# Second product of the last tile pair as seven block products, with the combined weights prepared through DRAM

## Chip, cores, metric

One core of one Trainium2 chip runs the whole kernel. The metric is the device time of one launch in microseconds (us), lower is better. Engines are named as in the profile: PE is TensorE (PEld its weight loads), DVE VectorE, ACT ScalarE, POOL GpSimd, SP the engine that issues most DMAs.

## What is computed

Masked attention (8 batches, 8 heads, 576 positions of 64) gives, rearranged, a matrix `x` of 4608 rows by 512. Behind it stands a feed-forward block:

```python
x = attn_out.transpose(0, 2, 1, 3).reshape(B * S, H * D)      # 4608 x 512
h = x @ w_in                                                  # 512 -> 2048
g = h * np.clip(h + 3.0, 0.0, 6.0) / 6.0
out = (g @ w_out).astype(np.float32)                          # 2048 -> 512
```

`h = x @ w_in` is called the first product here and `g @ w_out` the second. All arithmetic is float32. A float32 product is made of three matmuls on operands that are split into a high part and a remainder: high·high, high·low, low·high.

## The kernel before

The 4608 rows are nine tiles of 512: one for each batch (its first 512 positions), and one, called `l`, that gathers the last 64 positions of all eight batches. Tiles 0 to 2 are done one at a time (`ffn`). The other six are done in three pairs, (3, 4), (5, 6) and (7, `l`), by `ffn_pair`. `w_out` in its two parts lies in DRAM scratch as `wod` and is loaded again for each tile, 512 KB for each of its 16 row blocks `fc`.

**First product of a pair.** For each `m` of 0 to 7, `pair_products(m)` makes the blocks `fc` = 2m and 2m+1 of both tiles together. Two tiles times two blocks are a 2 x 2 block product, and it is made by seven block products in place of eight: sums of the two tiles (`combine_x`, tiles `xc`) and sums of weight blocks (`combine_weights`, DRAM scratch `wid`) are made ahead, and `product(0)` to `product(6)` run in two PSUM banks `ph`, with the sums between them taken while the accumulation goes on: `copy` takes a bank to SBUF, `add` adds a bank to such a copy, and the next product accumulates on the bank that was copied. Each product is two groups of three matmuls of 512 columns (lines 1210 to 1212). `gate` makes `g` from a bank or a copy with one ACT and one DVE instruction.

**Second product of a pair.** Tile a's is made between the first products (`second(fc, ...)`, `mm2`, lines 970 to 972): for each `fc`, four groups of three matmuls of 512 columns, one group for each block of 128 rows, in the four banks `acc`. Its operand `g` is split by ACT (line 1003) and POOL (line 1006). Tile b's `g` is kept in SBUF, and its second product follows alone, with the same number of matmuls.

In the last pair (`ends`), the last four `fc` of the second tile (`BEHIND`) are held back so that the four row blocks end one after the other; each is scaled by 1/6 out of its bank (`output`, lines 982 and 984) and stored.

**What sets the order.** No order is written out. `op(...)` records a step with its engine or engines, an estimated duration, the keys that it reads and writes and a due time; `Plan.emit` then goes through all steps as a list scheduler and writes each engine's instructions in the order it found. Each engine runs its list strictly in that order, DMA queues too. So a step that is added can move others on every engine that it shares.

Of the kernel before, what the change touches and what calls it, by code (L numbers as in the profile page):

```python
# [10 lines left out]
F32 = mybir.dt.float32  # L11
# [41 lines left out]
SHORT = 3.05  # L53
LASTS = (16.6, 2.8)
BEHIND = 4
PLAIN = {0: (0, 0), 1: (2, 0), 5: (2, 1)}
# [151 lines left out]
def attention_ffn(ctx: ExitStack, tc, q, k, v, w_in, w_out, out):  # L208
# [19 lines left out]
    wod = dp.tile([NFC, P, 2, TOK], F32, name="wod")  # L228
    wid = dp.tile([7 * NFC // 4, P, 2, TOK], F32, name="wid")

    plan = Plan()
# [744 lines left out]

    def output(t, i, uk, make, rows, due, ends=False):

# [7 lines left out]
        def store():  # L986
            o = tiles[uk.key if isinstance(uk, Slot) else uk]
            for n, (to, part) in enumerate(rows):
                (nc.scalar if ends and n % 2 else nc.sync).dma_start(to, o[part])
        op({"ACT": 0.6, "DVE": 0.69}, 0, ob, reads=[("acc", i), "tmps"] if isinstance(uk, Slot) else [("acc", i)], writes=[uk], take=uk if isinstance(uk, Slot) else None, due=due - 4000)  # L990
# [6 lines left out]

    def split_g(fc, uk, gk, due, t, held=False):
        def to(x):
            return tiles[gk[x]] if held else new(gp, gk[x], [P, TOK], F32R, f"g{x}{t}_{fc}")  # L1000

# [166 lines left out]

    def ffn_pair(p):
        s0 = first[p]  # L1170
        ends = p == len(PAIRS) - 1
        long, short = LASTS if ends else (LONG, SHORT)
        half = s0 + HALVES * long
# [3 lines left out]
        def out_of(which, end):  # L1177
            def go(i):
                uk = Slot(tmps)
                output(names[which], i, uk, lambda: None, rows_of(PAIRS[p][which], i), end, ends=ends and which == 1)  # L1180
            return go
# [13 lines left out]
        def pair_products(m):  # L1195
# [35 lines left out]

            def gate(fc, which, src, reads, give, both):
                if which:
                    uk = kept_g[fc]
                    make = lambda: new(xp, uk, [P, TOK], F32, f"g{p}_{fc}")
                else:
                    uk = u_slot()
                    make = lambda: new(gp, uk, [P, TOK], F32, f"u{p}_{fc}")
# [19 lines left out]
            gate(f1, 1, lambda: tiles[banks[0]], [banks[0]], None, False)  # L1258

        for m in range(HALVES):  # L1260
            if m:
# [4 lines left out]
        second(NFC - 1, half - 0.2 * long)  # L1266
        behind = NFC - BEHIND
        for fc in range(NFC):
            at = half + fc * short
            gk = [("g", fc % 2, x) for x in range(2)]  # L1270
            if ends and fc >= behind:
                gk = [("ge", fc, x) for x in range(2)]

                def both(fc=fc, gk=gk):
                    t = new(wp, xc[fc - behind], [P, 2, TOK], F32R, f"ge{fc}")
                    for x in range(2):
                        tiles[gk[x]] = t[:, x]
                op("SP", 0.0, both, writes=[xc[fc - behind], *gk], due=at)
            split_g(fc, kept_g[fc], gk, at - 2000, names[1], held=ends and fc >= behind)
            when = [at + 0.2 * i * short for i in range(4)]  # L1280
            if ends and fc >= behind:
                when = [half + (behind + BEHIND * 0.25 * i + 0.01 * (fc - behind)) * short for i in range(4)]
            mm2(fc, gk, second_weights(fc, half + min(fc, behind) * short), when.__getitem__, names[1], None, out_of(1, half + NFC * short))

# [66 lines left out]
    for p, now in enumerate(PAIRS):  # L1351
        combine_x(p, first[p] - 30)
        ffn_pair(p)
        for b in PAIRS[p + 1] if p + 1 < len(PAIRS) else ():
# [44 lines left out]
```

## Time and profile before

| | before |
|---|---|
| device time, median of 3 runs | 898.61 us (897.04 to 899.19) |
| the profiled execution: its own time | 896.24 us |
| its span in the trace | 894.5 us |
| PE busy | 874.2 us (98%) |
| weight loads (PEld) busy | 705.3 us (79%) |
| DVE, ACT, POOL busy | 522.9, 378.5, 430.4 us |
| DMA | 191.17 MB, 214 GB/s on average |
| chain that ended last | PE 83%, DMA 7%, SP's queue 3%, DVE 3% |

The profile shows one execution. Its times count from the start of the span; the launch's own time is 1.7 us longer. A matmul's recorded length (0.39 us for 512 columns) is longer than the distance from one start to the next, because matmuls are pipelined. So the rate is read from starts, and a short wait of PE can be seen as a wider distance of two starts while the engine still counts as busy.

### The profile page before, as it was taken

The numbers are of one execution on the slowest core, as the hardware profiler recorded it, in microseconds if no ns is written. First come the engines' busy times: TensorE is split into PE (matmuls) and PEld (weight loads), VectorE is DVE, ScalarE is ACT, GpSimd is POOL, SyncE is SP. The second block draws the span as 40 slices with busy tenths as digits, with TensorE's granted clock in tenths as the row PEclk, the third lists the DMA queues.
The fourth block names the chain that finished last, engine by engine and source line by source line (L and its number), as shares of the span: only waits on it lengthen the run. The fifth ranks groups of instructions, "written<-read, shape, count | busy, mean of one in ns | idle before, by whom it ended". The sixth has DMA issues, their size and how long they took to land.

```text
span 894.5 us, 19609 instructions
## 1 busy us (share of the span) xinstructions
PE 874.2 (98%) x7760; PEld 705.3 (79%) x7760; DVE 522.9 (58%) x910; ACT 378.5 (42%) x673; POOL 430.4 (48%) x389
## 2 busy tenths in 40 slices
PE   9899999999999999999999999999999999999997
PEld 6577868878887877878888888888887888888786
DVE  6778866577876867775768704444576024444400
ACT  4686555343434334444345623344355223223320
POOL 6778677286766757232334945122258422112340
PEclk9999999999999999999999999999999999999999
DMA  8989998778989889997973695866746676555364
GB/s 196 296 187 173 258 344 218 176 211 205 244 209 249 230 214 208 282 232 195 226 213 131 240 277 170 267 192 206 218 129 245 232 232 195 198 187 193 127 213 131
DMA packets 219290, 191.17 MB, mean 214 GB/s; under 512 B 163520, under 2 KB 177856, under 8 KB 219200
## 3 DMA queue, kind: packets, MB, share of 16 engines
q1 hardware_dynamic: 218724, 189.12, 75.3%
q8 instruction: 61, 1.00, 0.5%
q10 hardware_dynamic: 476, 0.82, 0.3%
q14 instruction: 29, 0.24, 0.1%
HBM read 157.38 MB, written 32.51 MB: 212 GB/s over the span
## 4 chain that ended last, share of the span: by engine, by line
PE 83%; DMA 7%; SPq 3%; DVE 3%; POOL 2%; ACT 1%; issue 1%; ACTq 0%; DVEq 0%; POOLq 0%
PE ph L1210 9%; PE ph L1212 8%; PE ph L1211 8%; PE ph L1037 4%; PE acc L970 4%; PE acc L972 4%; PE ph L1039 4%; PE acc L971 4%; PE ph L1038 4%; PE ps L667 3%; DMA rawi<-in_moe_w_in_dram 2%; SPq L413 2%; PE pv L432 2%; PE acc0b L970 2%; PE acc0a L970 2%; PE acc0b L972 2%
## 5 line engine op out<-in xcount | busy, mean ns | idle before, releaser
L1210 PE MATMUL ph<-xc,wi 128*128 128x512 f32 x336 | 132.9, 396 | 0.1
L1212 PE MATMUL ph<-xc,wi 128*128 128x512 f32 x336 | 130.9, 389 | 0.0
L1211 PE MATMUL ph<-xc,wi 128*128 128x512 f32 x336 | 130.9, 389 | 0.0
L1229 DVE TENSOR_TENSOR htmp<-ph,htmp 128x512 f32<-128x512 f32 x72 | 49.6, 689 | 78.0 <-PE ph L1212 72.8
L1006 POOL TENSOR_TENSOR g<-u,g 128x512 fp32r<-128x512 f32 x48 | 63.4, 1320 | 40.2 <-ACT g L1003 27.9
L1037 PE MATMUL ph<-x,wi 128*128 128x512 f32 x192 | 77.7, 405 | 3.5 <-DVE u L1076 3.2
L972 PE MATMUL acc<-wo,g 128*128 128x512 f32 x192 | 75.1, 391 | 2.3 <-POOL g L1006 2.3
L970 PE MATMUL acc<-wo,g 128*128 128x512 f32 x192 | 77.2, 402 | 0.0
L1039 PE MATMUL ph<-x,wi 128*128 128x512 f32 x192 | 75.2, 392 | 0.6 <-POOL wi L363 0.6
L1038 PE MATMUL ph<-x,wi 128*128 128x512 f32 x192 | 75.1, 391 | 0.0
L971 PE MATMUL acc<-wo,g 128*128 128x512 f32 x192 | 74.9, 390 | 0.0
L1210 PEld LDWEIGHTS ph<-xc,wi 128*128 128x128 f32 x336 | 63.0, 188 | 14.2 <-DVE g L1076 0.6
L1212 PEld LDWEIGHTS ph<-xc,wi 128*128 128x128 f32 x336 | 63.1, 188 | 13.4
L1211 PEld LDWEIGHTS ph<-xc,wi 128*128 128x128 f32 x336 | 63.1, 188 | 12.4
L799 DVE STREAM_TRANSPOSE atloc<-e 32x192 f32<-32x192 f32 x168 | 61.9, 368 | 8.9 <-POOL e L758 5.2
L743 POOL TENSOR_TENSOR e<-e,st 128x288 f32<-128x288 f32 (+1 forms) x30 | 34.3, 1143 | 62.2 <-DVE st L721 62.1
L1072 ACT ACTIVATE u<-ph,three 128x512 f32<-128x512 f32 x48 | 33.0, 688 | 73.4 <-PE ph L1039 72.2
L1072 ACT ACTIVATE u<-htmp,three 128x512 f32<-128x512 f32 x48 | 34.7, 723 | 66.7 <-DVE htmp L1229 66.7
L1006 POOL TENSOR_TENSOR g12a<-u,g02a 128x512 fp32r<-128x512 f32 x14 | 18.1, 1292 | 84.4 <-ACT g02a L1003 84.4
L1006 POOL TENSOR_TENSOR g11a<-u,g01a 128x512 fp32r<-128x512 f32 x16 | 21.4, 1335 | 69.5 <-ACT g01a L1003 68.1
L1221 ACT COPY htmp<-ph 128x512 f32<-128x512 f32 x53 | 31.1, 588 | 42.4 <-PE ph L1212 42.0
L758 POOL TENSOR_TENSOR e<-e,st 128x288 f32<-128x288 f32 (+1 forms) x30 | 35.5, 1183 | 26.2 <-DVE st L754 25.7
(234 smaller groups left out, 2092.2 us busy)
## 6 DMA issues: line engine op xcount, KB each, us to landing
wo<-wod SPq DMA_DIRECT2D x128, 512.0 KB
wi<-wid SPq DMA_DIRECT2D x84, 512.0 KB
rawi<-in_moe_w_in_dram SPq DMA_DIRECT2D x16, 512.0 KB
rawo<-in_moe_w_out_dram SPq DMA_DIRECT2D x16, 512.0 KB
wod<-wo SPq DMA_DIRECT2D x16, 512.0 KB
wid<-st SPq DMA_DIRECT2D x64, 128.0 KB
qn<-in_q_dram SPq DMA_DIRECT2D x112, 72.0 KB
kn<-in_k_dram SPq DMA_DIRECT2D x112, 72.0 KB
```

The costliest lines, as they stand in the source:

```text
L799: nc.vector.transpose(at[PAD * (a + h):PAD * (a + h) + PAD, :, PAD * a:PAD * a + PAD], e[PAD * a:PAD * a + PAD, :, PAD * h:PAD * h + PAD])
L970: nc.tensor.matmul(acc, gh, woh, start=fc == 0, stop=False)
L971: nc.tensor.matmul(acc, gh, wol, start=False, stop=False)
L972: nc.tensor.matmul(acc, gl, woh, start=False, stop=end)
L1006: on(e).tensor_tensor(out=to(1), in0=tiles[uk], in1=tiles[gk[0]].bitcast(F32), op=ALU.subtract)
L1037: nc.tensor.matmul(ph, wih, xh, start=n_ == 0, stop=False)
L1038: nc.tensor.matmul(ph, wih, xl, start=False, stop=False)
L1039: nc.tensor.matmul(ph, wil, xh, start=False, stop=n_ == NCC - 1)
L1072: nc.scalar.activation(make(), src(), AF.Relu, bias=three)
L1210: nc.tensor.matmul(ph, w[:, j, 0], x[:, 0], start=u in (0, 1, 3) and j == 0, stop=False, skip_group_check=u in (2, 4, 5, 6))
L1211: nc.tensor.matmul(ph, w[:, j, 0], x[:, 1], start=False, stop=False, skip_group_check=u in (2, 4, 5, 6))
L1212: nc.tensor.matmul(ph, w[:, j, 1], x[:, 0], start=False, stop=j == 1, skip_group_check=u in (2, 4, 5, 6))
```

## The change

Only the last pair's second product is computed in another way. `ffn_pair` gets an object `Last` for that pair, which also takes over its gates.

The two tiles' `g` blocks 2m and 2m+1 (`a11`, `a12` of tile 7, `a21`, `a22` of tile `l`) and the two halves of `w_out`'s 512 columns form a 2 x 2 block product over m. It is made by seven block products per m, each of 128 rows by 256 columns (`HALF`): `s1 = a21 + a22`, `s2 = s1 - a11`, `a11 - a21` and `s4 = a12 - s2` stand against matching sums of the weight halves. `products` issues three matmuls of 256 columns per block of 128 rows, four blocks per product and m.

- Three of the seven (`x`: a11, `z`: s1, `y`: s2) run beside the first products of the next m, in six banks (`acc` 0 to 3 and the two `s` banks): `live`.
- The other four (`b21`, `t3`, `t4`, `b22`) follow behind the first products: `rest`. The sums of the seven results are made while PE runs on (`add`, DVE reading a bank and SBUF), and each quarter of the output is stored as it is done. The last one, `b22`, ends block by block.
- The weight sums are made in `combine_out` during the pair before, for m = 0 to 7, 16 us apart by due time: `wod` is loaded into the free `xf` tiles of SBUF, added, mixed and split by POOL, DVE and ACT, and written to new DRAM scratch, `wtl` and `wtr`. SP issues ten DMAs for each m.
- All remainders of split operands in `Last` are made by DVE (`split`); before, POOL made nearly all.

```diff
-LASTS = (16.6, 2.8)
-BEHIND = 4
+LASTS = (13.9, 11.4)
+HALF = TOK // 2
+LAG = 4
...
+    wtl = dp.tile([HALVES, P, 2, 2, HALF], F32, name="wtl")
+    wtr = dp.tile([2, HALVES // 2, P, 2, 2, HALF], F32, name="wtr")
...
-    def ffn_pair(p):
+    def ffn_pair(p, last=None):
...
             def gate(fc, which, src, reads, give, both):
+                if last:
+                    last.gated(m, fc % 2, which, src, reads, give, due)
+                    return
...
+        if last:
+            last.begin()
+            for m in range(HALVES):
+                if m:
+                    last.live(m - 1, s0 + m * long)
+                pair_products(m)
+                last.sums(m, s0 + m * long - 2000)
+            last.live(HALVES - 1, s0 + HALVES * long, (0,))
+            last.rest(s0 + (HALVES + 0.1) * long)
+            return
...
+    def combine_out(m, due):
...
+            def load(i=i):
+                for x in range(2):
+                    nc.sync.dma_start(buf(2 * i + x), wod[2 * m + i, :, x])
+
+            def whole(e, i=i):
+                on(e).tensor_tensor(out=buf(2 * i), in0=buf(2 * i), in1=buf(2 * i + 1), op=ALU.add)
...
+            op({"POOL": 1.3, "DVE": 0.69}, 0, whole, reads=[keys[2 * i + 1]], writes=[keys[2 * i]], due=due, port=True)
...
+            def put(c=c):
+                for x in range(2):
+                    if c == 0:
+                        nc.sync.dma_start(wtl[m, :, :, x], buf(x).rearrange("p (t n) -> p t n", t=2))
+                    else:
+                        for w in range(2):
+                            nc.sync.dma_start(wtr[w, m // 2, :, m % 2, x], buf(c + x, w))
...
+            mix(s1, a21, a22, ALU.add, "s1")
+            mix(s2, s1, a11, ALU.subtract, "s2")
+            mix(a21, a11, a21, ALU.subtract, "")
+            mix(s4, a12, s2, ALU.subtract, "")
...
+            op("ACT", 0.63, hi, reads=[src], writes=[gk[0]], due=due)
+            op("DVE", 0.69, lo, reads=[src, gk[0]], writes=[gk[1]], due=due, port=True)
...
+        def products(self, banks, blocks, gk, wk, at, begin, end, due, take=None):
...
+                    nc.tensor.matmul(to, gh, wh, start=begin and i % 2 == 0, stop=False, skip_group_check=True)
+                    nc.tensor.matmul(to, gh, wl, start=False, stop=False, skip_group_check=True)
+                    nc.tensor.matmul(to, gl, wh, start=False, stop=end, skip_group_check=True)
...
-        ffn_pair(p)
+        ffn_pair(p, Last(p) if p == len(PAIRS) - 1 else None)
+        for m in range(HALVES if p == len(PAIRS) - 2 else 0):
+            combine_out(m, first[p] + 30 + 16 * m)
```

How the order moves, at the two places that the prediction speaks of.

**PE in the last pair, m = 1, from the last group of `product(2)` to the first of `product(4)`.** Both write the bank `ph_1_0`; `ph_1_1` and `ph_1_3` are the other bank. Before:

```order
L1210 MATMUL ph_1_0_8691<-xc_2_8322,wi_8421 128x512
L1211 MATMUL ph_1_0_8691<-xc_2_8322,wi_8421 128x512
L1212 MATMUL ph_1_0_8691<-xc_2_8322,wi_8421 128x512
L970 MATMUL acc2a_8639<-wo_8590,g02a_8700 128x512 [waits DMAHW4_49]
L971 MATMUL acc2a_8639<-wo_8590,g02a_8700 128x512
L972 MATMUL acc2a_8639<-wo_8590,g12a_8706 128x512 [waits Pool_49]
L1210 MATMUL ph_1_3_8728<-xc_3_8125,wi_8650 128x512 [waits DMAHW3_49,DVE_49]
L1211 MATMUL ph_1_3_8728<-xc_3_8125,wi_8650 128x512
L1212 MATMUL ph_1_3_8728<-xc_3_8125,wi_8650 128x512
L1210 MATMUL ph_1_0_8691<-xc_4_8143,wi_8650 128x512 [waits Activation_49]
```

With the change:

```order
L1212 MATMUL ph_1_0_8847<-xc_2_8505,wi_8542 128x512
L1213 MATMUL ph_1_0_8847<-xc_2_8505,wi_8542 128x512
L1214 MATMUL ph_1_0_8847<-xc_2_8505,wi_8542 128x512
L1212 MATMUL ph_1_1_8875<-xc_1_8433,wi_8542 128x512
L1213 MATMUL ph_1_1_8875<-xc_1_8433,wi_8542 128x512
L1214 MATMUL ph_1_1_8875<-xc_1_8433,wi_8542 128x512
L1212 MATMUL ph_1_0_8847<-xc_4_8248,wi_8633 128x512 [waits DVE_49]
```

Between the two groups on `ph_1_0`, while the bank is copied out, two groups of three matmuls stood on PE before, and one stands there now; the order is the same for m = 2 to 7. The copy is ACT's before and DVE's now.

**POOL during the pair before (5, 6), around the remainders `g11a` that PE waits for.** `L1006` (now `L1009`) makes such a remainder, `L743` and `L758` (now `L746`, `L761`) belong to attention, and `L1302`, `L1307`, `L1314` are `combine_out`'s add, mixes and remainders on the `xf` tiles (`hxf`). Before:

```order
L1006 TENSOR_TENSOR g11a_7275<-u_3_7259,g01a_7269 128x512 [waits PE_49,Activation_49]
L743 TENSOR_TENSOR e<-e,st_2_7347 128x2x8x18 [waits DVE_49]
L758 TENSOR_TENSOR e<-e,st_2_7347 128x2x8x18 [waits DVE_49,Activation_49]
L1006 TENSOR_TENSOR g11a_7400<-u_4_7376,g01a_7392 128x512 [waits PE_49,Activation_49,Pool_49]
L1006 TENSOR_TENSOR g11a_7482<-u_5_7431,g01a_7473 128x512 [waits PE_49,Activation_49,Pool_49]
```

With the change:

```order
L1009 TENSOR_TENSOR g11a_7294<-u_3_7268,g01a_7287 128x512 [waits PE_49,Activation_49]
L1302 TENSOR_TENSOR hxf_2084<-hxf_2084,hxf_2093 128x512 [waits DMAHW7_49,DMAHW4_49,DMAHW0_49]
L746 TENSOR_TENSOR e<-e,st_2_7385 128x2x8x18 [waits DVE_49]
L1302 TENSOR_TENSOR hxf_2117<-hxf_2117,hxf_2130 128x512 [waits DMAHW3_49,DMAHW2_49,DMAHW1_49]
L1009 TENSOR_TENSOR g11a_7427<-u_4_7379,g01a_7419 128x512 [waits PE_49,Activation_49,Pool_49]
L1307 TENSOR_TENSOR hxf_2093<-hxf_2117,hxf_2093 128x256 [waits DMAHW5_49,DVE_49,Pool_49]
L761 TENSOR_TENSOR e<-e,st_2_7385 128x2x8x18 [waits DVE_49]
L1307 TENSOR_TENSOR hxf_2130<-hxf_2117,hxf_2093 128x256 [waits Pool_49]
L1314 TENSOR_TENSOR hxf_2093<-hxf_2093,hxf_2084 128x512 [waits Activation_49,Pool_49]
L1314 TENSOR_TENSOR hxf_2130<-hxf_2130,hxf_2117 128x512 [waits DVE_49,Activation_49]
L1009 TENSOR_TENSOR g11a_7515<-u_5_7446,g01a_7507 128x512 [waits PE_49,Activation_49]
```

Steps of `combine_out` now stand between the remainders, the adds among them waiting for a DMA to land.

## Rows read from the trace of the kernel before

**Rows 1.** Windows over the whole kernel's later part: start and end of the stretch, its length, busy time of PE, PEld, DVE, ACT and POOL with their instructions, granted PE clock (1.00 is the upper of its two levels, 2.4 GHz), mean DMA share, GB/s. The first product of pair (5, 6) begins at 502 us, that of pair (7, `l`) at 682 us; 180 to 340 us is where `combine_weights` runs.

```profile
core 0: us, PE busy (x) PEld busy (x) DVE busy (x) ACT busy (x) POOL busy (x), PEclk, DMA share, GB/s
363.00:400.00 37.00, 37.00 (x331) 29.74 (x331) 25.93 (x50) 18.58 (x34) 11.03 (x9) 1.00 0.99 264
502.00:682.00 180.00, 179.20 (x1263) 146.85 (x1262) 90.46 (x142) 77.16 (x131) 74.04 (x55) 1.00 0.70 214
682.00:889.80 207.80, 206.36 (x906) 169.27 (x904) 61.66 (x88) 58.29 (x91) 62.68 (x48) 1.00 0.60 198
180.00:250.00 70.00, 69.41 (x982) 56.01 (x965) 54.78 (x109) 26.40 (x52) 50.30 (x46) 1.00 0.84 216
250.00:340.00 90.00, 86.78 (x853) 69.65 (x852) 67.54 (x111) 36.60 (x67) 60.98 (x52) 1.00 0.87 232
```

**Rows 2.** Waits of PE from 502 us to the end: who waited for whom, total, times, longest.

```profile
PE acc1a L972 <- POOL g11a L1006: 0.8, 1, 0.8
PE acc2b L970 <- DVE htmp L984: 0.8, 1, 0.8
PE acc2b L970 <- DMA wo<-wod: 0.3, 1, 0.3
PE acc2a L972 <- DVE g12a L1006: 0.2, 1, 0.2
```

**Rows 3.** Groups of instructions on PE: the matmuls of the last pair's second product, tile 7 (`acc2a`) and tile `l` (`acc2b`, the last four blocks as `ge`). Lines 971 and 972 have a row of the same count for each of these.

```profile
L970 PE MATMUL acc2a<-wo,g02a 128*128 128x512 f32 x64 | 24.9, 389 | 0.0
L970 PE MATMUL acc2b<-wo,g02b 128*128 128x512 f32 x48 | 18.8, 391 | 0.8 <-DVE htmp L984 0.8
L970 PE MATMUL acc2b<-wo,ge 128*128 128x512 f32 x16 | 6.3, 396 | 0.3 <-DMA wo<-wod 0.3
```

**Rows 4.** Timeline of the last pair's first products (start, length, engine, line, operation): twelve matmuls lie between the first and the last of these PE rows, and the DVE row is the copy of the bank that the row above it ended.

```profile
743.07 0.39 PE L1212 MATMUL ph<-xc,wi 128*128 128x512 f32 x1
...
743.50 0.69 DVE L1223 COPY htmp<-ph 128x512 f32<-128x512 f32 x1 [0.79 <-PE ph L1212]
...
745.79 0.39 PE L1212 MATMUL ph<-xc,wi 128*128 128x512 f32 x1
```

**Rows 5.** Timeline, all engines, in tile 6's second product: a matmul and the load for the next one.

```profile
700.01 0.39 PE L970 MATMUL acc1b<-wo,g01b 128*128 128x512 f32 x1
700.01 0.19 PEld L971 LDWEIGHTS acc1b<-wo,g01b 128*128 128x128 f32 x1
...
700.24 0.39 PE L971 MATMUL acc1b<-wo,g01b 128*128 128x512 f32 x1
```

**Rows 6.** Timeline at the kernel's start: short float32 matmuls with loads of 128 columns, merged (first start, length of all, count). L690's alternate between two halves of the array's rows.

```profile
6.00 0.58 PEld L533 LDWEIGHTS kp<-ident,kn 72*128 72x128 f32 x8 [0.76 <-DMA kn<-in_k_dram]
...
10.24 0.97 PEld L690 LDWEIGHTS ps<-kplain,qt 64*128 64x128 f32 x16 [0.24 <-issue]
10.24 1.11 PE L690 MATMUL ps<-kplain,qt 64*128 64x72 f32 x16
```

**Rows 7.** Groups: mean length of the loads in rows 5 and 6, and of the matmuls of L690 (last figure ahead of the bar, ns).

```profile
L690 PE MATMUL ps<-kplain,qt 64*128 64x72 f32 x32 | 2.2, 279 | 0.0
L971 PEld LDWEIGHTS acc2a<-wo,g02a 128*128 128x128 f32 x64 | 12.0, 188 | 2.5
L533 PEld LDWEIGHTS kp<-ident,kn 72*128 72x128 f32 x32 | 2.3, 142 | 1.1 <-DMA kn<-in_k_dram 0.8 <-issue 0.3
L690 PEld LDWEIGHTS ps<-kplain,qt 64*128 64x128 f32 x32 | 1.9, 187 | 0.5 <-issue 0.5
```

**Rows 8.** Timeline in the last pair at m = 1: a gate on DVE, the PE group that waits for it, and the next matmuls.

```profile
736.97 0.69 DVE L1076 SCALAR_TENSOR_TENSOR g<-g,ph 128x512 f32<-128x512 f32 x1 [0.48 <-ACT g L1072]
737.18 0.39 PE L1212 MATMUL ph<-xc,wi 128*128 128x512 f32 x1
...
737.72 0.50 PE L1210 MATMUL ph<-xc,wi 128*128 128x512 f32 x1
738.06 0.40 PE L1211 MATMUL ph<-xc,wi 128*128 128x512 f32 x1
738.30 0.39 PE L1212 MATMUL ph<-xc,wi 128*128 128x512 f32 x1
```

**Rows 9.** Two of the waits of rows 2 in the timeline of PE, with the start before and after each.

```profile
841.44 0.39 PE L971 MATMUL acc2a<-wo,g02a 128*128 128x512 f32 x1
842.06 0.50 PE L972 MATMUL acc2a<-wo,g12a 128*128 128x512 f32 x1 [0.23 <-DVE g12a L1006]
842.40 0.40 PE L970 MATMUL acc2a<-wo,g02a 128*128 128x512 f32 x1
...
882.03 0.39 PE L972 MATMUL acc2b<-wo,ge 128*128 128x512 f32 x1
882.67 0.50 PE L970 MATMUL acc2b<-wo,ge 128*128 128x512 f32 x1 [0.25 <-DMA wo<-wod]
883.01 0.40 PE L971 MATMUL acc2b<-wo,ge 128*128 128x512 f32 x1
```

**Rows 10.** Groups on ACT, DVE and POOL: a high part, a remainder on POOL, a remainder on DVE while POOL works in SBUF too, and DVE reading a bank of 288 columns.

```profile
L1003 ACT CAST g02a<-u 128x512 fp32r<-128x512 f32 x16 | 9.9, 620 | 29.7 <-PE acc2a L971 25.9 <-PE acc1b L971 2.1 <-DVE u L1076 1.7
L1006 POOL TENSOR_TENSOR g12a<-u,g02a 128x512 fp32r<-128x512 f32 x14 | 18.1, 1292 | 84.4 <-ACT g02a L1003 84.4
L1149 DVE TENSOR_TENSOR xc<-hxf,xc 128x512 fp32r<-128x512 f32 x15 | 19.3, 1292 | 2.1 <-ACT xc L1146 1.8
L547 DVE COPY kplain<-kp 128x288 f32<-128x288 f32 x3 | 1.3, 437 | 2.7 <-PE kp L533 2.7
```

**Rows 11.** Timeline at the end: the last matmul and the last scaling out of a bank. The span ends at 894.5 us.

```profile
889.38 0.39 PE L972 MATMUL acc2b<-wo,ge 128*128 128x512 f32 x1
889.80 0.60 ACT L982 ACTIVATE htmp<-acc2b 128x512 f32<-128x512 f32 x1 [4.84 <-PE acc2b L972]
```

More of the change, by code (lines that the diff above doesn't have):

```diff
@@ L975, in mm2, with output @@
                 out_of(i)
-    def output(t, i, uk, make, rows, due, ends=False):
+    def output(t, i, uk, make, rows, due):
         def ob(e):
@@ L987, in store @@
             o = tiles[uk.key if isinstance(uk, Slot) else uk]
-            for n, (to, part) in enumerate(rows):
-                (nc.scalar if ends and n % 2 else nc.sync).dma_start(to, o[part])
+            for to, part in rows:
+                nc.sync.dma_start(to, o[part])
         op({"ACT": 0.6, "DVE": 0.69}, 0, ob, reads=[("acc", i), "tmps"] if isinstance(uk, Slot) else [("acc", i)], writes=[uk], take=uk if isinstance(uk, Slot) else None, due=due - 4000)
@@ L996, in rows_of, with split_g @@
         return [(out[(2 * i + x) * S + TOK:(2 * i + x + 1) * S, :], slice(x * LEFT, (x + 1) * LEFT)) for x in range(2)]
-    def split_g(fc, uk, gk, due, t, held=False):
+    def split_g(fc, uk, gk, due, t):
         def to(x):
-            return tiles[gk[x]] if held else new(gp, gk[x], [P, TOK], F32R, f"g{x}{t}_{fc}")
+            return new(gp, gk[x], [P, TOK], F32R, f"g{x}{t}_{fc}")
         def hi():
@@ L1167, in combine_x @@
             split(5, (0, 1))
-    def ffn_pair(p):
+    def ffn_pair(p, last=None):
         s0 = first[p]
-        ends = p == len(PAIRS) - 1
-        long, short = LASTS if ends else (LONG, SHORT)
+        long, short = LASTS if last else (LONG, SHORT)
         half = s0 + HALVES * long
@@ L1179, in go @@
                 uk = Slot(tmps)
-                output(names[which], i, uk, lambda: None, rows_of(PAIRS[p][which], i), end, ends=ends and which == 1)
+                output(names[which], i, uk, lambda: None, rows_of(PAIRS[p][which], i), end)
             return go
@@ L1266, in ffn_pair @@
         second(NFC - 1, half - 0.2 * long)
-        behind = NFC - BEHIND
         for fc in range(NFC):
@@ L1270, in ffn_pair @@
             gk = [("g", fc % 2, x) for x in range(2)]
[L1271 to L1275, printed above, removed]
+            split_g(fc, kept_g[fc], gk, at - 2000, names[1])
+            when = [at + 0.2 * i * short for i in range(4)]
+            mm2(fc, gk, second_weights(fc, at), when.__getitem__, names[1], None, out_of(1, half + NFC * short))
@@ L1276, in both @@
                     for x in range(2):
                         tiles[gk[x]] = t[:, x]
[L1278 to L1283, printed above, removed]
+                op("SP", 0.0, make, writes=[xc[4 + m], *gk], due=need - 1000)
@@ new lines, in rest @@
+                gks.append(self.split(order[3][2](m), need + m * 0.1 - 1500, gk=gk))
+                if m % 2 == 0:
+                    wks.append(order[3][3](m, need))
+            for i in range(4):
+                for m in range(HALVES):
+                    self.products(banks, (i,), gks[m], wks[m // 2], m % 2, m == 0, m == HALVES - 1, need + (i + m / HALVES) * 0.25 * long)
+                key = add(banks[i // 2], keep["u4"][i // 2], keep["u4"][i // 2], part=i % 2)
+                store(0, 1, key, (i,), split=True)
```

191 lines of the change are left out of this document (added).

## The prediction

> **What bounds the kernel now.** I read the windows first. In the stretches of the last two pairs PE is busy for 179.2 of 180 us and 206.4 of 207.8 us at the full granted clock, 1.00, while DVE, ACT and POOL work a third to a half of the time and DMA 0.60 to 0.70 [rows 1]. Then the waits of PE: from 502 us to the end there are four, 2.1 us together [rows 2]. So PE's issue of matmuls sets the time of these stages, and other engines matter only where they make it wait. The rate comes from starts in the timeline, not from recorded lengths: twelve matmuls of 512 columns take 745.79 - 743.07 = 2.72 us, 0.2267 us each [rows 4], though each is recorded with 0.39.
>
> **Matmuls removed and added.** The last pair's second product is 3 x (64 + 48 + 16) = 384 matmuls of 512 columns [rows 3], so 384 x 0.2267 = 87.1 us. The change issues 7 products x 8 m x 4 row blocks x 3 = 672 matmuls of 256 columns. Columns fall by an eighth, but there are 1.75 times as many instructions and weight loads, so what counts is the distance of two starts at 256 columns, which this trace does not have. Bounds: if all of 0.2267 goes with the columns, half of it, 0.113 us, and 76.2 us in all. At the clock of 2.4 GHz, 512 columns are 0.2133 us, which leaves 0.0133 us that may be the same for each matmul: then 256 columns take 0.1067 + 0.0133 = 0.120 us, 80.6 us in all. If it counts twice, once for the matmul and once for its load, 0.133 us and 89.6 us, 2.5 us more than before. I take 0.120, **-6.4 us** (ends -10.9 and +2.5).
>
> Is the weight load in the way? It is recorded with 0.188 us [rows 7], longer than 0.120. But a recorded load is not the distance of two loads. At the start of the kernel eight loads of 128 columns take 0.58 us [rows 6], and as one is 0.142 long [rows 7], they start every (0.58 - 0.142) / 7 = 0.063 us. The L690 loads, 0.187 us long, come as 16 matmuls in 1.11 us, less their 0.279 us: one every 0.055, each half of the array every 0.11 us [rows 6, 7]. That is just under 0.120, so I let the load hide. Loads do run beside a matmul here: the load for the next one starts with the running one, on all 128 rows [rows 5].
>
> The Trainium skill (TensorE: Matmul & The Clock Gate, section Back-to-back issue gap) gives N/2.4 + 2.5 ns for a warm gap: 216 ns at 512 columns, where rows 4 show 227, so the measurement decides; by that rule the change would save 384 x 0.2158 - 672 x 0.1092 = 9.5 us instead of 6.4, an estimate from that page.
>
> **Waits that go.** A wait costs its recorded time and a slower restart. From 841.44 to 842.40 PE needs 0.96 us for two steps worth 0.45, so the wait recorded as 0.23 costs 0.51; the one at 882 costs 0.98 - 0.45 = 0.53 [rows 9]. Recorded time plus 0.28, then, and the third one in the last pair, 0.8 [rows 2], costs 1.08. All three stand in work that is replaced: the evacuation of `acc2a` ahead of `acc2b`, a late remainder, a late `wo`. **-2.1 us.**
>
> **Waits that come, in the first products.** Between the last group of `product(2)` and the first of `product(4)` the bank is copied out. Two other groups stood there, 1.36 us; now there is one, 0.68. From the start of a group's last matmul to the copy's start it is 743.50 - 743.07 = 0.43 us, the copy takes 0.69 [rows 4], and PE starts 0.06 after DVE is done (736.97 + 0.69 to 737.72) [rows 8]: 1.18 us, where PE could go on after four steps, 0.91. That is a wait of 0.27 and a restart of 0.11 (0.34 between the next two starts instead of 0.23 [rows 8]), 0.38 us, for m = 1 to 7. At m = 1 the copy after `product(0)` has six matmuls of 256 columns as cover, 0.72 us, and costs about the same. 8 x 0.39 = **+3.1 us**. The ends are 0, if the copy goes faster than these rows say, and twice that, if the other short cover, `gate` before `product(1)`, fails as well, as it does in rows 8.
>
> The rest of this stage fits. In 9.5 us of first products and 36 x 0.120 = 4.3 us of new ones, 13.8 us for each m, DVE has 13 steps (copies, adds, gates, a mix and the three remainders that were POOL's), at 0.69 us 9.0 us; if the four in SBUF are stretched to 1.29, as where POOL works there too [rows 10], 11.4. POOL's three mixes at 1.29 are 3.9, ACT's load is smaller still.
>
> **Behind the first products.** Each 12 new matmuls, 1.44 us, need one high part (0.62, ACT [rows 10]) and one remainder (0.69 on DVE, since POOL is idle by then). The banks of one product are evacuated while another runs in others. Two places are tight by my count along DVE's order, the first use of a `ph` bank and the second remainder of `t3`; I put **+0.6 us** there, ends 0 and the 2.1 that this stretch loses now. Weight traffic is as before, 512 KB for every 2.9 us against one for each 12 matmuls of 0.2267, 2.7 us.
>
> **The end.** The last step is a scaling of 256 columns instead of 512. It is 0.60 us now [rows 11]; DVE takes 0.44 for 288 columns [rows 10], so **-0.2 us**, and the 4.1 us from there to the end of the span stay.
>
> **The pair before, where the weights are made.** `combine_out` adds for each m two adds, four half mixes, two high parts, two remainders and ten DMAs of SP, 2 MB read and written, 16.8 MB in all. In the last pair 198 GB/s are a DMA share of 0.60 [rows 1], so 330 GB/s at full share: 51 us more in about 180, and the share rises from 0.70 to about 0.98. A stretch of 0.99 DMA share from 363 us on costs PE nothing, 37.00 of 37.00 us, since weights are due 14 us ahead. On the other side stands the stretch where `combine_weights` ran: there PE lost 3.8 of 160 us [rows 1]; the same rate over 8 x 16 us would be 3.1. DVE has 90 of 180 us here and gets some 15 more, nearer to the stretch without loss. I take **+0.8 us**, ends 0 and 3.1.
>
> **Sum:** -6.4 - 2.1 + 3.1 + 0.6 - 0.2 + 0.8 = -4.2 us. The profiled execution took 896.24 us, which gives 892.0; it is 2.4 us faster than the median of the three runs, and I expect the change's median to stand as that of before does: 898.61 - 4.2 = **894.4 us**.
>
> **Rivals.**
> - *Full proportion.* 256 columns take 0.113 us: 4.5 us better, 889.9. For it: no row separates a fixed part. Against: the load's 0.11 us per half array and 0.0133 us per matmul that the clock does not explain. 0.13.
> - *DVE late.* DVE now makes every remainder and both copies. If one step for each m slips behind another in its order, a second wait of 0.39 comes to 8 x 0.39 = 3.1 us, 897.5, no measurable change. For it: remainders on DVE of 1.29 us beside POOL [rows 10]. Against: 2 to 5 us free for each m. 0.17.
> - *POOL held by the scratch loads (slower).* POOL's adds in `combine_out` wait for a DMA from DRAM and stand ahead of the remainders `g11a` in POOL's order. A load that lands late holds POOL, and PE stops at the `g11a` behind it, as it did once for 0.8 us [rows 2], which costs 1.08. Once in each of the eight rounds, that is 8.6 us in place of my 0.8: 894.4 + 7.8 = 902.2. It decides the sign from a hold of this size in about seven rounds. For it: a DMA share near 1. Against: DMA reached 0.99 before without a wait, and eight loads may be under way. 0.13.
> - *The load bounds (slower).* If a load of 128 rows does not run beside a matmul on the same rows, or its recorded 0.188 is its distance, 256 columns cost 0.188 + 0.013 = 0.201 us: 135.1 us, 54.5 more than I count, 948.9. Rows 5 and 6 speak against both. 0.03. The Trainium skill (the same page, section Measured speedup vs the span model) says that a load overlaps a running matmul only where the row groups differ; rows 5 do not bear it out.
> - That the change does not save columns is excluded: its order holds the 672 short matmuls and none of the 384.
>
> **How the numbers follow.** My forecast has 0.50, other mishaps 0.04. What can be told from no change is 0.3%, 2.7 us: below 895.9 is faster, above 901.3 slower. Of the forecast 0.45 lie below 895.9; with full proportion and a little of the rest, faster 0.60. The rest of the forecast, DVE late and a few holds of POOL make 0.24 the same; the two slower rivals and mishaps 0.16 slower. The range goes from 888.5, where full proportion meets fewer new waits than counted, to 901.5, all but the worst of POOL's holds. The forecast's own range is 891.5 to 897.
>
> **What would show it.** In the profile after: starts of 256-column matmuls 0.120 us apart (the first term; 0.113 or 0.133 would move it by 4.5 up or 9 down); distances of 0.5 us ahead of `product(4)` for m = 1 to 7; no wait of PE on POOL's `g11a` above 1 us between 502 and 682 us, with the DMA share near 0.98 there; the stretch behind the first products about 46 us long. I am wrong if PE waits on POOL or on DMA in the pair (5, 6), or if the 256-column matmuls stand further apart than 0.13 us.

## The result: 0.7% slower, and the profile after

The changed kernel takes **903.0 us** (median of 14 runs, 899.06 to 910.14); the kernel before has 898.15 (14 runs, 893.83 to 902.39). The ratio is 1.007, 95% interval 1.0041 to 1.0099: slower by 5 to 6 us (4.9 from median to median, 6.3 by the ratio), where I had forecast 894.4. The profiled execution took 900.29 us, its span is 898.4. Three of all the executions reported here, one each of e5, e7 and e15, were over 1.5% longer than the fastest of the same kernel; the medians hold them, the ratios leave them out.

Starts in the timelines divide the two spans:

| stretch | before | after | difference |
|---|---|---|---|
| up to the first matmul of the pair (5, 6) | 502.4 | 501.9 | -0.5 |
| from there to the last pair's first matmul | 179.9 | 189.1 | **+9.2** |
| from there to the start of the last matmul | 207.1 | 204.0 | -3.1 |
| from there to the end of the span | 5.1 | 3.4 | -1.7 |

The last pair and the end of the span gained 4.8 us; the pair before, whose matmuls did not change, lost nearly twice that. The windows of the profile after, columns as in [rows 1]:

```profile
502.00:560.00 58.00, 58.00 (x346) 47.64 (x345) 22.63 (x32) 22.07 (x38) 37.55 (x29) 1.00 0.87 260
560.00:620.00 60.00, 56.82 (x392) 46.37 (x391) 27.98 (x45) 24.21 (x42) 23.41 (x22) 0.97 0.90 264
620.00:691.00 71.00, 67.39 (x531) 53.96 (x529) 52.12 (x77) 37.79 (x66) 51.58 (x42) 1.00 0.86 276
691.00:740.00 49.00, 49.00 (x209) 40.31 (x210) 19.89 (x22) 14.64 (x25) 31.83 (x25) 0.97 0.92 325
```

PE lost 3.2 us of 60 and 3.6 of 71 from 560 to 691 us, and in two of the stretches the granted clock is below 1.00 (0.97). The waits of PE from 502 us on, which answer to [rows 2]:

```profile
PE ph L1212 <- issue: 3.2, 1, 3.2
PE ph L1212 <- DMA wi<-wid: 2.6, 2, 2.3
PE ph L1212 <- DVE htmp L1231: 0.8, 1, 0.8
PE az L1432 <- DVE gm L1395: 0.6, 1, 0.6
```

The first three lines are new and lie in the pair (5, 6) or at its end. The longest, put down to "issue", is none of an engine or a weight. In the timeline it stands behind a burst of 128 small matmuls of the attention:

```profile
580.06 1.27 PE L670 MATMUL ps<-kplain,sq 64*32 64x18 f32 x128
584.51 0.50 PE L1212 MATMUL ph<-xc,wi 128*128 128x512 f32 x1 [3.18 <-issue]
...
586.06 0.63 PE L1212 MATMUL ph<-xc,wi 128*128 128x512 f32 x1
586.49 0.63 PE L1213 MATMUL ph<-xc,wi 128*128 128x512 f32 x1
```

The burst and its loads are 256 instructions in 1.27 us. PE's instructions come by DMA too, on queue q8 in packets of 16 KB. The DMA view of narrow windows shows when this packet started (queue, packets, MB, busy share of the 16 engines). Before (burst at 579.31), from 578 to 580 us, DMA 38% busy:

```profile
q1 hardware_dynamic: 88, 0.29, 37.9%
q8 instruction: 1, 0.02, 2.9%
```

After, from 578 to 580 us no such packet and DMA full; it came between 581.5 and 583.5, behind the burst:

```profile
q1 hardware_dynamic: 350, 0.80, 105.0%
```
```profile
q1 hardware_dynamic: 294, 0.78, 102.8%
q8 instruction: 1, 0.02, 3.4%
```

So PE had run out of instructions. The packet's own record says the same: before, it started at 578.86 us, 0.45 ahead of the burst; after, at 581.99, and PE went on 1.43 us after its end. 1.4 us after PE restarted the clock was at its lower level, 1.2 GHz: the rows of 0.63 us stand 0.43 apart instead of 0.227, for 3.4 us, which costs 1.6. The second long wait, for a weight, was followed by the same:

```profile
690.99 0.50 PE L1212 MATMUL ph<-xc,wi 128*128 128x512 f32 x1 [2.34 <-DMA wi<-wid]
...
691.82 0.63 PE L1212 MATMUL ph<-xc,wi 128*128 128x512 f32 x1
692.25 0.63 PE L1213 MATMUL ph<-xc,wi 128*128 128x512 f32 x1
```

This weight had little to spare before as well. Its load, before and after:

```profile
677.04 0.42 SPq L956 DMA_DIRECT2D wi<-wid  x1
```
```profile
684.98 0.43 SPq L959 DMA_DIRECT2D wi<-wid  x1
```

Before, it was issued 5.3 us ahead of PE's matmul at 682.33 and landed (the last of its landing marks in the trace) after 4.7, 0.6 us ahead. After, it was issued 3.7 us before PE came to that matmul and took 6.0: the wait of 2.3 is 1.6 from the later issue and 1.3 from the slower landing, less the 0.6.

Why issues came late shows in what SP waited for from 502 to 740 us. Before:

```profile
SPq L956 <- PE ph L1212: 46.0, 22, 6.5
SPq L945 <- PE acc1a L972: 40.8, 13, 9.2
SPq L945 <- PE acc1b L972: 34.0, 16, 3.2
SPq L945 <- PE acc0b L972: 30.0, 12, 4.1
```

After:

```profile
SPq L948 <- PE acc0b L975: 28.0, 13, 4.1
SPq L959 <- PE ph L1214: 18.8, 9, 8.6
SPq L948 <- PE acc1b L975: 15.4, 7, 4.4
SPq L948 <- PE acc1a L975: 13.0, 6, 6.0
...
SPq L948 <- DMA wi<-wid: 5.2, 3, 3.4
...
SPq L1299 <- DMA wtl<-hxf: 3.6, 4, 2.8
```

Before, SP waited 156 us for PE in all (151 in these lines): it was ahead, and most loads went out as soon as PE had freed their buffer. After, its waits for PE are 86 us (75 in the lines shown), and some 30 kinds of wait for DMA, ACT, POOL and DVE stand between. Of the pair's 22 `wi` loads from 564 us on, 3 were issued some 1 us or more after their buffer was free; now 13 of the 22 from 561 us on. From issue to the last of its landing marks in the trace a `wi` took 4.2 us (median, 560 to 620 us), now 6.8.

### The profile page after: what moved, and what is told of

It is laid out like the page before. It is cut to its first block, busy times and chain, and to the rows that moved or that the text cites. A ratio compares the mean times of both kernels' runs of the same rounds, so it can differ in the third digit from the quotient of the medians.

```text
span 898.4 us, 20510 instructions
## 1 busy us (share of the span) xinstructions
PE 873.8 (97%) x8048; PEld 716.6 (80%) x8048; DVE 594.5 (66%) x1001; ACT 400.7 (45%) x716; POOL 471.2 (52%) x425
## 4 chain that ended last, share of the span: by engine, by line
PE 77%; DMA 10%; DVE 4%; POOL 3%; SPq 2%; issue 2%; ACT 1%; DVEq 0%; POOLq 0%; ACTq 0%
PE ph L1212 8%; PE ph L1214 8%; PE ph L1213 8%; PE ph L1040 4%; PE ph L1042 3%; PE acc L973 3%; PE ph L1041 3%; PE acc L975 3%; PE acc L974 3%; PE az L1432 3%; PE az L1430 3%; PE az L1431 3%; PE ps L670 3%; DMA v<-in_v_dram 2%; DMA kn<-in_k_dram 2%
## 5 line engine op out<-in xcount | busy, mean ns | idle before, releaser
L1212 PE MATMUL ph<-xc,wi 128*128 128x512 f32 x336 | 135.5, 403 | 7.6 <-issue 3.2
L1213 PE MATMUL ph<-xc,wi 128*128 128x512 f32 x336 | 132.1, 393 | 0.0
L1214 PE MATMUL ph<-xc,wi 128*128 128x512 f32 x336 | 132.1, 393 | 0.0
L1009 POOL TENSOR_TENSOR g<-u,g 128x512 fp32r<-128x512 f32 x48 | 63.5, 1322 | 41.8 <-ACT g L1006 30.8
L746 POOL TENSOR_TENSOR e<-e,st 128x288 f32<-128x288 f32 (+1 forms) x30 | 34.4, 1147 | 61.4 <-DVE st L724 61.3
L1079 DVE SCALAR_TENSOR_TENSOR u<-u,ph 128x512 f32<-128x512 f32 x48 | 32.9, 685 | 24.4 <-ACT u L1075 23.3
L761 POOL TENSOR_TENSOR e<-e,st 128x288 f32<-128x288 f32 (+1 forms) x30 | 36.2, 1207 | 23.5 <-DVE st L757 23.5
L1040 PEld LDWEIGHTS ph<-x,wi 128*128 128x128 f32 x192 | 36.0, 188 | 11.4 <-DVE u L1079 2.8
L975 PEld LDWEIGHTS acc<-wo,g 128*128 128x128 f32 x192 | 36.1, 188 | 11.0 <-POOL g L1009 3.2
```

The lines of the kernel that those rows point to most:

```text
L975: nc.tensor.matmul(acc, gl, woh, start=False, stop=end)
L1009: on(e).tensor_tensor(out=to(1), in0=tiles[uk], in1=tiles[gk[0]].bitcast(F32), op=ALU.subtract)
L1040: nc.tensor.matmul(ph, wih, xh, start=n_ == 0, stop=False)
L1212: nc.tensor.matmul(ph, w[:, j, 0], x[:, 0], start=u in (0, 1, 3) and j == 0, stop=False, skip_group_check=u in (2, 4, 5, 6))
L1213: nc.tensor.matmul(ph, w[:, j, 0], x[:, 1], start=False, stop=False, skip_group_check=u in (2, 4, 5, 6))
L1214: nc.tensor.matmul(ph, w[:, j, 1], x[:, 0], start=False, stop=j == 1, skip_group_check=u in (2, 4, 5, 6))
```

## Experiments

The loss moves a little from execution to execution, and the part ahead of 502 us too (the first matmul of the pair (5, 6) starts at 500 to 509 us). So the table has, beside the times of all runs, the distance **D** from this matmul to the start of the last one, in the one profiled execution: the same matmuls in all but the first and third row, whose last pair is that of before. D is of one execution: in e8 and e18 of the slowest of the kernel, in e12 nearly of the fastest. Seven of the kernels (e1, e3 to e5, e12 to e14) leave work out.

| kernel | us, median | ratio to before, 95% | D, us |
|---|---|---|---|
| before | 898.15 | 1 | 386.9 |
| the change | 903.0 | 1.0041 to 1.0099 | 393.1 |
| e2 before + sums | 906.93 | 1.0057 to 1.0154 | 395.0 |
| e1 no sums | 892.39 | 0.9925 to 0.9983 | 383.1 |
| e3 sums' arithmetic alone | 895.5 | 0.9952 to 1.0011 | 383.7 |
| e4 sums' transfers alone | 901.75 | 1.0015 to 1.0061 | 393.5 |
| e5 80 transfers of half size | 900.64 | 0.9995 to 1.0068 | 389.9 |
| e14 40 transfers of full size | 893.97 | 0.9952 to 0.9996 | 384.3 |
| e12 loads alone | 895.83 | 0.9952 to 1.0 | 384.7 |
| e13 stores alone | 902.9 | 1.005 to 1.0106 | 392.4 |
| e6 sums 28 us apart | 906.82 | 1.0074 to 1.0142 | 392.5 |
| e7 sums by ACT's queue | 907.44 | 1.0054 to 1.0148 | 397.7 |
| e8 sums 100 us later | 904.37 | 1.0059 to 1.0117 | 394.1 |
| e9 last weights early | 902.01 | 1.0024 to 1.0077 | 391.3 |
| e10 gap at the burst | 901.28 | 1.0021 to 1.008 | 388.9 |
| e11 both | 903.17 | 1.003 to 1.0078 | 391.5 |
| e15 sums in 32 DMAs | 902.69 | 1.0039 to 1.0086 | 392.0 |
| e16 32 DMAs, early weights | 900.05 | 1.0008 to 1.0057 | 387.4 |
| e17 32 DMAs, gap | 898.61 | 0.9993 to 1.0041 | 388.3 |
| e18 32 DMAs, both | 898.19 | 0.9965 to 1.0024 | 391.1 |

**Which stage: e1 and e2.**

```diff
 # e1: no call; the last pair loads wod blocks for wtl, wtr
-        for m in range(HALVES if p == len(PAIRS) - 2 else 0):
-            combine_out(m, first[p] + 30 + 16 * m)
 # e2: the kernel before with combine_out and this call
```

> The change without the weight sums: nothing is read, added or written for them in the pair (5, 6), and the last pair reads plain blocks of the same size in their place (the sums are left out, so the products are not the reference's). Theory: the loss stands in the pair before, where weights and instructions come late; without the sums the last pair's gain of about 6 us is left: 890 to 894 us, no wait of PE over 1 us between 502 and 682 us, clock 1.00 there. Rival (the loss is in the last pair's block products): 900 us or more.

> The kernel before, with the weight sums of the change made in the pair (5, 6) and never read. Theory: the loss stands there whatever the last pair does: 905 to 911 us, 7 to 13 us over before, with PE waits of several us between 560 and 700 us and the clock at half after the long ones. Rival (the loss is in the last pair's products): within 2 us of before. My forecast's term was +0.8 us.

Both as the theory has it. Without sums the pair (its first matmul to the last pair's first) takes 179.8 us as before; with them 188.3, though its last pair is the old one. PE in e1, 560 to 691 us, and the busy share of DMA, 0.78 and 0.61:

```profile
560.00:620.00 60.00, 60.00 (x468) 49.28 (x470) 27.32 (x45) 24.25 (x41) 11.67 (x10) 1.00 0.78 230
620.00:691.00 71.00, 70.22 (x513) 57.43 (x499) 49.60 (x74) 35.39 (x60) 35.95 (x27) 1.00 0.61 192
```

**Arithmetic or transfers: e3 and e4.**

```diff
 # e3: without the ops load and put;  e4: without whole, mix, hi, lo
```

> The change with the sums' adds, halves, high parts and remainders on what lies in the buffers, without their loads and stores; the last pair reads plain blocks (the sums are not made). Theory, transfers: 890 to 895 us, since without the 16.8 MB the weights come in time. Rival, engines: DVE, POOL and ACT are held by the added steps and the copies out of the banks come late: 900 us or more.

> The change with the sums' 80 DMAs, without their arithmetic (what is loaded is stored again, so the sums are not made). Theory, transfers: 899 to 906 us, as the change itself. Rival, engines: 890 to 895 us. In between, 896 to 898 us, if half of it is SP waiting in order for the arithmetic ahead of its stores.

The transfers: 188.4 us for the pair, the arithmetic 180.6 (its time, 895.5, is half a us above the range). By the ratios e1 and the change are some 10 us apart; the transfers alone make 7.5 of them and the arithmetic alone 2.4, each uncertain by 3 us or so. In e4 DMA is full, and both long waits are there without any step on POOL or DVE:

```profile
560.00:620.00 60.00, 57.91 (x396) 47.31 (x395) 25.20 (x43) 22.36 (x39) 10.55 (x10) 0.97 0.98 300
620.00:691.00 71.00, 66.62 (x521) 53.09 (x520) 46.48 (x71) 33.27 (x56) 33.13 (x24) 0.98 0.98 311
```
```profile
PE ph L1212 <- DMA wi<-wid: 3.7, 1, 3.7
PE ph L1212 <- issue: 2.1, 1, 2.1
```

**Bytes, number or direction: e5, e12, e13, e14.**

```diff
 # e5: e4 with rows [:64];  e14: e4 with "for x in range(1)"
 # e12: e4 without put;  e13: e4 without load
```

> As the transfers alone, with the same 80 DMAs but half the rows in each (64 of 128), so half the bytes; the sums are not made and the last pair reads plain blocks. With the transfers alone the stretch from the pair's first matmul to the last pair's first took 188.4 us instead of 179.9. If bytes on the DMA engines cause it: under 183 us there, since the busy share of 560 to 691 us falls from 0.98 to near 0.8, and 893 to 897 us in all. If it is the number of DMAs (SP's issues in order, their places among those under way): about 188 us there and 900 to 903 us in all.

> The transfers alone, but every second one left out: 40 DMAs of full size, so the same bytes as with half the rows in 80 DMAs (which took 185.1 us in the pair, 900.6 in all); the sums are not made, the last pair reads plain blocks. If the bytes count: 185 us again. If the number of DMAs in SP's order counts: 181 to 183 us, and 892 to 897 us in all.

> The sums' 32 loads alone, 8.4 MB, read into their buffers and not used; no arithmetic, no stores (the sums are not made; the last pair reads plain blocks). The transfers alone, loads and stores, made 8.6 us in the pair (188.4 us against 179.8 without sums). If every byte counts alike: 183 to 185 us. If the stores are what delays the others: under 181 us, and 891 to 894 us in all.

> The sums' 48 stores alone, 8.4 MB, of what lies in the buffers; no loads, no arithmetic (the sums are not made). If every byte counts alike: 183 to 185 us for the pair. If the stores are what delays the others: 186 to 188 us, and 898 us or more in all. If the loads are: under 181 us.

Half the bytes in 80 DMAs (e5) left D 6.8 us over e1, in 40 (e14) or 32 (e12) 1.2 and 1.6; by the ratios 7.0, 1.8 and 2.0. The pair took 185.1, 181.0 and 181.4 us: e14 speaks for the number, e5 lies between the two ranges and e12 between "every byte alike" and "the stores". Nor is e5 the number alone: with half the rows in each DMA, DMA was 0.95 busy for 268 GB/s from 560 to 620 us, in e14 0.91 for 275. In e14 and e12 only the burst's wait is left, shorter, and the clock holds:

```profile
PE ph L1213 <- issue: 0.9, 1, 0.9
```
```profile
PE ph L1212 <- issue: 1.2, 1, 1.2
```

e13 settles no direction: with no loads to wait for, all 48 stores were issued between 498 and 556 us (DMA share 1.02 from 502 to 560), and PE waited there for `wo` and `wi`.

**Another place or queue: e6, e7, e8.**

```diff
-            combine_out(m, first[p] + 30 + 16 * m)
+            combine_out(m, first[p] + 30 + 28 * m)   # e6;  e8: first[p] + 130 + 16 * m
 # e7: combine_out's nc.sync.dma_start as nc.scalar.dma_start
```

> The change with the sums of one m due 28 us after the last instead of 16, so that the same 16.8 MB and the same steps are spread over some 225 us, the last three m beside the last pair's first products. If a full DMA causes the loss: the wait in front of 584 us and the one at 691 us shrink or go, 181 to 184 us for the pair (5, 6), and 893 to 898 us in all. If any transfer of these queued ahead of a weight load costs: the same 8 to 9 us, partly in the last pair, 900 to 904 us.

> The change with the 80 DMAs of the sums issued by ACT instead of SP; bytes and steps as in the change. If SP's order is the cause (weight loads stand behind loads and stores that wait): the weight loads start right when their buffer comes free again, 181 to 184 us for the pair (5, 6), and 893 to 898 us in all. If the bytes are the cause: 187 us or more there, 900 us or more. ACT then waits in order for what it stores, so copies out of banks can come late, which would make it slower still.

> The change with all sums due 100 us later, from about 632 to 752 us, behind the attention of this pair: same density, other place. If a full DMA causes the loss where the attention's transfers run too: no wait at 584 us, 180 to 184 us for the pair (5, 6) up to its second products; the second products have a DMA share of about 0.7 and get 0.3 more, so a wait of 1 to 3 us may come there: 893 to 899 us in all. If the loss follows the sums wherever they stand: 900 to 905 us.

All three failed; none is faster than the change. In e6 DMA was about as full around the burst (0.87 from 560 to 620 us) and the wait for instructions stayed at 3.2 us, so it does not test that cause; the wait at the last pair's first matmul went (0.1 us left), and waits for ACT (2.2 us) and POOL (1.6) came. In e7 the wait for the weight stayed at 2.3 us and the one for instructions went; ACT, in order behind its stores, copied banks late (5.4 us of PE's waits for `htmp`), and DMA was as full (0.90 from 560 to 620). The Trainium skill (DMA: Bandwidth & Descriptors, section Issuing engines are not separate DMA queues) says that DMAs run on the same 16 engines whichever engine starts them; this run agrees. In e8 both long waits went, as expected, but POOL now had the sums beside the remainders that the second products wait for:

```profile
PE acc1b L975 <- POOL g11b L1009: 2.6, 2, 1.6
```

**The two long waits, one by one: e9, e10, e11.**

```diff
-    def first_weights(n, need):
+    def first_weights(n, need, ahead=30):
...
-        op("SP", 0.45, load, ..., due=need - 14, early=need - 30, after=1.4)
+        op("SP", 0.45, load, ..., due=need - 14, early=need - ahead, after=1.4)
...
-                loaded[v // 2] = first_weights(v // 2, need)
+                loaded[v // 2] = first_weights(v // 2, need, 50 if last else 30)   # e9
...
-            combine_out(m, first[p] + 30 + 16 * m)
+            combine_out(m, first[p] + (6 if m < 2 else 36) + 16 * m)   # e10;  e11: both
```

> The change, with the weight loads of the last pair's first products let into SP's order 50 us ahead of their due time instead of 30; nothing else. In the change the first of them is issued at 684.98 us, 21.5 us after its buffer is free, behind loads that wait for PE, and lands at 691. If SP's order is what makes PE wait at 691 us: that wait (2.3 us) and the half clock behind it (1.6 us) go, the wait at 584 us stays; 185 to 186 us from the pair's first matmul to the last pair's first, and 4 us less than the change: 897 to 901 us. If the full DMA makes every load late whatever its place: no change, 901 to 905 us.

> The change, with the sums of the first two m due 24 us earlier and the others 6 us later, so that none of their DMAs runs from about 560 to 582 us, ahead of the burst of 128 small matmuls at 580 us; nothing else. If the fetch of PE's instructions is what the sums' transfers delay there: it starts ahead of the burst again, the wait of 3.2 us and the half clock behind it (1.6 us) go, the one at 691 us stays; 184 to 186 us for the pair and 4 to 5 us less than the change: 896 to 900 us. If that wait has another cause: 901 to 905 us.

> Both edits together. If the two waits with their half clock are the loss: no PE wait over 1.5 us between 502 and 700 us, 180 to 182 us for the pair, and 892 to 896 us in all, under before by 1 to 4 us. If what delays one only moves on to the next weight load: 898 us or more.

e9 took its wait away: the load went out at 668.33 us, and PE does not wait at the last pair's first matmul. But others came (1.6 us for `g11a`, 1.1 for a copy), and the forecast of 4 us less failed. e10 took the pair's time that it was to take (185.7 us), but not the time in all. Its list of waits has none for "issue". Yet the wait is there, shorter, under another name:

```profile
582.58 1.27 PE L670 MATMUL ps<-kplain,sq 64*32 64x18 f32 x128
...
584.35 0.39 PE L1214 MATMUL ph<-xc,wi 128*128 128x512 f32 x1
584.79 0.45 DVE L724 TENSOR_REDUCE st<-e 128x16 f32<-128x288 f32 x1
585.99 0.50 PE L1212 MATMUL ph<-xc,wi 128*128 128x512 f32 x1 [1.25 <-DVE st L724]
```

The three matmuls behind the burst ran, then PE stood for 1.25 us. The profile names DVE's `st`, which these matmuls do not read and which had ended 0.75 us before. The packet of instructions started at 583.65, behind the burst's first matmul by 1.07 us, and ended 1.23 us before PE went on. From 567 to 589 us no DMA of the sums was issued, but the pair's own loads, put off by them, kept DMA full (99.4% from 580 to 584). What the edit took away is 2 us of the wait and the half clock behind it; here too others came (1.5 us for `g11a`, 0.9 for a copy).

Together (e11) they gave nothing more, as the rival had it; that execution came to the burst at 585.18 us, past the gap, and waited 1.9 us for its instructions. The times of e9 and e10 cannot be told from the change's.

**Fewer, larger DMAs: e15 to e18.**

```diff
-        halve([wkey("o", 2, c)], [("xf", i, c) for i in range(2)])
+        halve([wkey("o", 2, c)], [("xf", c // 2, 2 * (c % 2) + i) for i in range(2)])
...
+                nc.sync.dma_start(tiles["whole", wkey("o", 2, 2 + i)], wod[2 * m + i])
...
+                nc.sync.dma_start(wtr[m // 2, :, m % 2] if c else wtl[m], tiles["whole", wkey("o", 2, 2 + c // 2)])
```

> The change with the sums' buffers side by side, so that each m loads two whole blocks and stores two, 32 DMAs of 512 KB in the pair (5, 6) instead of 80 of 128 and 256 KB; the same 16.8 MB, the same arithmetic, one load more for each m in the last pair. If the number of DMAs in SP's order makes most of the loss (half the bytes in 80 DMAs cost 5.3 us in the pair, in 40 DMAs 1.2): 182 to 185 us for the pair and 895 to 899 us in all, 4 to 8 us under the change. If the bytes do: 188 us again, 901 to 905 us.

> The same 32 DMAs, and the last pair's first weight loads let in 50 us ahead, so that they don't stand behind the sums. If a wait at the start of the last pair is left in the run with 32 DMAs, it goes, and 893 to 897 us; if none is left, the same time as that run within 2 us.

> The same 32 DMAs, and none of them from about 560 to 582 us, ahead of the burst of small matmuls. If the late fetch of PE's instructions is left in the run with 32 DMAs: it goes here, 3 to 5 us under that run, 892 to 896 us. If it is not left there: the same time within 2 us.

> 32 DMAs, the last pair's first weight loads 50 us ahead, and the gap ahead of the burst, all together. If the three pieces of the loss add up, 384 to 386 us from the pair's first matmul to the end of matmuls (393.1 in the change, 386.9 before, 383.1 without sums) and 893 to 896 us in all, faster than before. If the loss moves to the next wait each time, as with the first two edits together: 387 us or more and 897 to 901 us, no faster than before.

Number alone is not it either: e15 still waits 3.2 us for instructions, with the clock at half for 6.8 us, and is no faster than the change; its wait for the weight is gone, but there the order moved too (the last pair's first matmul starts at 698 us). With the other edits the loss shrinks: the wait for instructions is 2.7 us in e16, 1.3 in e17 and 1.7 in e18. e18 takes the time of before, ratio 0.9994, so the pieces did not add up to a gain. No version tried beats before, apart from those that leave work out.

## Why the prediction was wrong

- *Matmuls removed and added, -6.4.* Right. In the timeline after, 256 columns stand 0.120 us apart, and three quarters of their distances are that to the nanosecond:

```profile
892.32 0.28 PE L1431 MATMUL az<-wt,ge 128*128 128x256 f32 x1
892.33 0.19 PEld L1432 LDWEIGHTS az<-wt,ge 128*128 128x128 f32 x1
892.44 0.28 PE L1432 MATMUL az<-wt,ge 128*128 128x256 f32 x1
```

That settles the rival *The load bounds* as well: the loads, recorded with 0.19 us on the same 128 rows, run beside the matmuls. (The sentence on loads that the prediction takes from the Trainium skill stands on the page that it names, TensorE: Matmul & The Clock Gate, but in the section The mechanism; these rows do not bear it out either.)

- *Waits that go, -2.1.* Right: none of the three is left.
- *Waits that come, +3.1.* Right in kind and nearly in size. Ahead of `product(4)` two starts are 0.49 us apart, then 0.34; over twice 0.227 that is 0.38 us, at m = 1 to 7, 2.6 in all, and the place at m = 1 behind six new matmuls costs 0.34:

```profile
820.27 0.39 PE L1214 MATMUL ph<-xc,wi 128*128 128x512 f32 x1
820.76 0.50 PE L1212 MATMUL ph<-xc,wi 128*128 128x512 f32 x1
821.10 0.39 PE L1213 MATMUL ph<-xc,wi 128*128 128x512 f32 x1
```

- *Behind the first products, +0.6.* Right: one wait of 0.6, for the remainder `gm` on DVE.
- *The end, -0.2.* Too small. I took the 4.1 us from the last scaling to the end as given [rows 11], but the last store has half the columns too, and is one DMA in place of two (which of the two counts, no run shows). After, the scaling ends at 895.70 and the span at 898.4, 2.7 us:

```profile
894.96 0.28 PE L1432 MATMUL az<-wt,ge 128*128 128x256 f32 x1
895.28 0.42 DVE L1478 SCALAR_TENSOR_TENSOR keepu<-az,keepu 128x256 f32<-128x256 f32 x1 [1.01 <-PE az L1432]
```

- *The pair before, +0.8, ends 0 and 3.1.* **This is the step that failed.** It measured +9.2 in the profile: 3.2 for late instructions, 2.3 for a late weight, 1.6 for the clock behind the first, and the rest in shorter waits and restarts; the clock behind the second, 1.6 more, fell into the last pair. Without the sums (e1) the other terms came out near their sum, -5.0: D fell by 3.8 us and the tail by 1.7, the median's ratio is 0.9954. I counted the DMAs' time as free up to a full share, on two grounds, and neither holds. One was the stretch of 0.99 DMA share without loss [rows 1]. It has short matmuls, but no burst like this one: its longest run in the timeline before is 144 instructions with the loads, where the burst has 256.

```profile
376.16 0.97 PE L667 MATMUL ps<-kplain,qplain 64*32 64x64 f32 x72
```

The other, that weights are due 14 us ahead, is the plan's figure: the load of the last pair's first weight, shown above, had 0.6 us to spare already before. The share itself came out under the forecast, 0.87 from 502 to 691 us against 0.98; what counted was where DMA was full, and that SP issues in order, so that a weight load stands behind sums that wait. And no term had the clock.

Of the rivals, *POOL held by the scratch loads* came to 902.2 us, close to 903.0, but by another mechanism: in the profile after no wait of PE is put down to POOL's `g11a`. Such waits of over 1 us came only where sums or weight loads were moved (e8, e9, e10 and e17, 1.5 to 2.1 us). What would show me wrong was named, a wait of PE on DMA in the pair (5, 6); that instructions come by DMA, and could be what is late, was not.

Shown: the stage, the transfers as the larger part, and the two long waits. The one for the weight goes when its load is let in earlier (e9). The one for instructions goes where DMA is not full ahead of the burst (e1, e3, e7, e8), and a gap in the sums alone only shortens it (e10). Open: why a full DMA holds the packet of instructions up for over 2 us, why other waits came when one was taken away, and what divides the loss between bytes and number; half of both together cost little, either alone did not settle it.

## To carry to other kernels

A DMA share under 1 over a stretch (0.87 here) does not make added transfers free: look in the trace at how long before its use each load lands, at how far ahead the in-order issuing engine is of its consumers (what it waits for), and at which loads pass the added ones. Bursts of short instructions are places where the instruction stream itself must have arrived; keep DMA from being full ahead of them. And a wait of a few us can cost, beside what it shows, a time at half clock. A wait's name in the profile is an inference: when the engine named had long been done, look for what else came just before PE went on.

## What the runs showed of the hardware

PE's instruction packets stand in the trace as DMA of a queue of its own. In 14 kernels (the change, e2, e4 to e6, e9 to e12, e14 to e18) DMA was full in the 3 us ahead of the burst at 576 to 587 us (share 0.99 to 1.11), and the packet started 0.8 to 3.4 us after the burst's first matmul. In all 14, PE stood for 0.9 to 3.2 us ahead of the same instruction, counted from the start of its list, and went on 1.2 to 1.5 us after the packet's end. Before and in e1, e3, e7 and e8 the share there was 0.65 to 0.81, the packet started between 0.8 us before the burst's start and 0.8 after, and PE did not wait. In e13 DMA was full and the packet late (2.9 us after), but in its order 28 matmuls of 512 columns, 6 us, stand between the burst and that instruction, and PE did not wait either.

With or behind waits of over 2 us the clock often fell to 1.2 GHz, after 10 of 14 such waits in these traces: for 3.4 us at a cost of 1.6, in e7 and e15 for 6.8 us; in e16 it did not after 2.7. Much of the difference between the medians goes with it. The mean granted clock of the change's 14 executions is 0.9913, that of 25 executions of before (those beside e1) 0.9948, and among the change's 14 a clock lower by 0.001 goes with 0.8 us more: 0.0035 makes some 3 of the 5 to 6 us, an estimate from these figures.
